# Order and pacing of an interleaved last stage: a convolution stream woven into a feed-forward network on one core

## The chip, the cores and the metric

The kernel runs on one core of one Trainium2 chip. The metric is device microseconds from one execution of the whole program; the kernel before took 1118.28 us (median of 3 runs, 1117.45 to 1119.73). The engines are named as in the profile: PE (TensorE), DVE (VectorE), ACT (ScalarE), POOL (GpSimd), SP (SyncE, which here only issues DMAs).

## What is computed

With S = 2048 positions, D = 576 channels and Dff = 4608, all in float32:

```python
xn  = layernorm(q)                          # over the 576 channels
h   = relu(xn @ w1) @ w2                    # feed-forward, 576 -> 4608 -> 576
kv  = shift_conv4(k, shift_k) * v           # 4-tap causal convolution per channel
y   = causal_conv(kv, ssm_k) + kv * ssm_D   # 2048 taps per channel, by a Fourier transform
out = q + xn * y + h
```

## The kernel before

**Two programs in one.** The feed-forward network (FFN) is the main loop, and the convolution is a generator, `conv()`, whose steps are issued in between. Positions are cut into 16 tiles t of 128 rows; four tiles make a block b, two blocks a half. Dff is cut into 12 chunks of 384, and each half goes through all of them, so that chunk numbers ci run from 0 to 11 for the first half (tiles 0 to 7) and from 12 to 23 for the second (tiles 8 to 15).

**The FFN.** Per chunk and block, `mm1` (L304) makes three hidden tiles of 128x512 with 14 matmuls each into the PSUM pool `psh` (two buffers); ACT writes the rounded relu `hh` (L319) and DVE the remainder `ll` (L320). `mm2` (L323) makes, for each of the four tiles, two products of 128x288 with 9 matmuls each into the PSUM pool `pso` (three buffers). DVE adds each product to `acc[t]`, which starts as x, in one operation that multiplies by `rstd` on the way (L337): xn is only centred before the matmuls (`centred`, L185), and the scale comes late, which relu allows. Weights come by SP (L267 to L282) and are split into a rounded and a rest part by ACT and POOL (L289, L297, L262). `make_xT` (L237) takes statistics on DVE, centres x, transposes it on PE into the PSUM pool `psf` (three buffers, shared with the convolution) and splits it. For block 2 it works in place.

**The convolution**, in four stages, each with an SBUF pool of its own; the matmuls of all of them write to `psf`:
- `fk`: first transform of the filter (L369), 32 units, to DRAM as zk.
- `fx`: four taps and a gate on DVE (L454 to L463), first transform of the result (L369), to DRAM as zx.
- `fm`: spectral product, 32 groups. For each group: k's transform (6 matmuls, L533), four copies by ACT for each half of the columns (L556 to L559); x's transform (6 matmuls), two `sw` copies by ACT (L583, L584) and a product by DVE for each half (L585), then a second product (L587) and the sum (L563); `yh` on ACT (L564) and `yl` on DVE (L566); and, a group later, the inverse transform (6 matmuls) and `vo` on ACT (L573), stored to DRAM as zy (L578). Inputs are split into `hi` by ACT and `lo` by DVE (L523, L524).
- `fo`: last transform. For tile t and u = 0, 1: load of zy (L598), `ohi` by ACT (L617) and `olo` by DVE (L618), two matmuls for each half of the columns (L657, L658), a copy by ACT (L659) and a sum by DVE (L660) into y. Then `gate(t)` multiplies by the centred x (L625) and `add(t)` scales by rstd and adds (L632): for tiles 0 to 7 to the saved first half (`fin` in DRAM) and straight to the output, on POOL's DMA queue; for tiles 8 to 15 into `acc[t]`, which the FFN of the second half is still adding to. The first transform of zy for any tile needs every group's store.

**What sets the order.** `tick` (L685) is called twice in each `mm1` and `mm2` with the matmul columns just issued. It adds `rate * cost` to a balance and, when the balance is not negative and no pause runs, takes one step of the generator; the step's weight (W_FK, W_FX, W_FM, W_FO) is taken off the balance. `rate` is the total weight of the convolution over `SHARE` of the FFN's columns less pauses (L678). At the first of the last chunk's sums in the second half, `rest_of_stream` (L343) issues whatever is left. A scheduler then places these instructions on the engines' queues: each engine runs its own queue strictly in the order given, and an instruction on the same tile as an earlier issued one waits for it. So the *issue* order decides who must wait for whom, and the scheduler, which takes what it holds to be ready, where each instruction stands on its engine.

**The start.** 22 matmuls on zeros (L715) run on PE while x and the first weights arrive; then come the transposes of the first four tiles (L231) and the first `mm1`.

Of the kernel before, what the change touches and what calls it, by code (L numbers as in the profile page):

```python
# [10 lines left out]
F32 = mybir.dt.float32  # L11
F32R = mybir.dt.float32r
AF = mybir.ActivationFunctionType
OP = mybir.AluOpType
# [24 lines left out]
GR = P // (2 * A2)  # L39
NG = A1 // GR  # L40
N_WARM = 22


W_MM1 = 14 * 512
# [63 lines left out]
def h3_ffn_kernel(ctx: ExitStack, tc, x, k, v, shift_k, ssm_k, ssm_D, w1, w2, fwd, inv, mid, out):  # L108
# [76 lines left out]
    def centred(dst, src, t):  # L185


        return nc.vector.tensor_scalar(dst, src, mv[:, t, 0:1], None, op0=OP.subtract)
# [20 lines left out]
    def first_xT(srcs):  # L209

        xT_tiles(0)
        ps = []
        for c in range(5):
            ps.append(ps_o.tile([P, 512], F32, tag="o", name=f"psx{c}") if c >= 3 else fft_psum())
        neg = xp.tile([P, BT], F32, tag="neg", name="neg", bufs=1)
        behind = None
        for t in range(BT):
            if t % 2 == 0:
                pair = xp.tile([P, 2, D], F32, tag="xn", name=f"xn{t}", bufs=BT // 2)
            xn = pair[:, t % 2, :]  # L220
            with tc.issue_after(behind.ins) if behind else nullcontext():
                stats(t, srcs[t])
                if t % 2 == 0:
                    behind = nc.vector.tensor_scalar(neg[:, t:t + 1], mv[:, t, 0:1], -1.0, None,
                                                     op0=OP.mult)
                    nc.scalar.activation(xn, srcs[t], AF.Identity, bias=neg[:, t:t + 1])
                else:
                    behind = centred(xn, srcs[t], t)
            for c in range(5):
                w = min(P, D - c * P)  # L230
                nc.tensor.transpose(ps[c][:w, t * P:(t + 1) * P], xn[:, c * P:c * P + w], ident)  # L231
        for c in range(5):
            split_x(0, c, ps[c])
        with tc.issue_after(done["dve"].ins):
            inv_std(0, BT)

    def make_xT(b, srcs, in_place=False):  # L237

        xT_tiles(b)
        t0 = b * BT  # L240
        with tc.issue_after(done["dve"].ins):
            for t in range(t0, t0 + BT):
                stats(t, srcs[t])
# [56 lines left out]
        return last  # L300

    hid = {}

    def mm1(ci, b, j):  # L304
        h1, l1, _, _ = weights[ci][j]
# [17 lines left out]
    def mm2(ci, b, i):  # L323
        t = b * BT + i
        cols = slice(i * P, (i + 1) * P)
        for h in range(2):
            ps = ps_o.tile([P, 512], F32, tag="o", name=f"pso{ci}_{t}_{h}")
            dc = slice(h * NH, (h + 1) * NH)
            n = 0
            for j in range(FT):  # L330
                hh, ll = hid[ci, b, j]
                _, _, h2, l2 = weights[ci][j]
                for a, m in ((hh, h2), (hh, l2), (ll, h2)):
                    nc.tensor.matmul(ps[:, :NH], a[:, cols], m[:, dc],  # L334
                                     start=n == 0, stop=n == 3 * FT - 1)
                    n += 1
            done["acc"] = nc.vector.scalar_tensor_tensor(  # L337
                acc[t][:, dc], ps[:, :NH], rstd[:, t:t + 1], acc[t][:, dc],
                op0=OP.mult, op1=OP.add)
# [12 lines left out]


# [25 lines left out]
    def conv():  # L379
# [212 lines left out]
        with tc.tile_pool(name="fo", bufs=2) as fp:  # L592
            raw, parts, rest, ys = {}, {}, {}, {}

            def load_z(t, u):
                if t < T:
                    raw[t, u] = fp.tile([P, D], F32, tag="zt", name=f"zo{t}_{u}", bufs=4)
                    nc.sync.dma_start(raw[t, u], zy[:, T * u + t, :])  # L598

            def load_rest(t):  # L600
                if t < T:
# [8 lines left out]
                    rest[t] = w, xt, ft  # L610

            def split(t, u):
                if t < T:
                    hi = fp.tile([P, D], F32R, tag="hi", name=f"ohi{t}_{u}", bufs=3)
                    lo = fp.tile([P, D], F32R, tag="lo", name=f"olo{t}_{u}", bufs=3)
                    with here():
                        nc.scalar.activation(hi, raw[t, u], AF.Copy)  # L617
                        nc.vector.tensor_tensor(lo, raw[t, u], hi, OP.subtract)  # L618
                    parts[t, u] = hi, lo

            def gate(t):

                if t >= 0:
                    with here():
                        nc.vector.scalar_tensor_tensor(ys[t], rest[t][1], mv[:, t, 0:1], ys[t],  # L625
                                                       op0=OP.subtract, op1=OP.mult)

            def add(t):
                if t >= 0:
                    to, more = (ys[t], rest[t][2]) if t < HT else (acc[t], acc[t])  # L630
                    with here():
                        nc.vector.scalar_tensor_tensor(to, ys[t], rstd[:, t:t + 1], more,  # L632
                                                       op0=OP.mult, op1=OP.add)
                    if t < HT:
                        move(to, out, t, store=True, queues=(nc.gpsimd, nc.gpsimd))

            units = [(t, u) for t in range(T) for u in range(U)]
            for n in range(3):
                load_z(*units[n])
            for t in range(2):  # L640
                load_rest(t)
            yield -PAUSE
            split(0, 0)
            yield -PAUSE / 8
            for n, (t, u) in enumerate(units):
                w = rest[t][0]
                hi, lo = parts[t, u]
                own, other = halves(u)
                if u == 0:
                    ys[t] = fp.tile([P, D], F32, tag="y", name=f"y{t}", bufs=3)  # L650
                low = fp.tile([P, D], F32, tag="low", name=f"low{t}_{u}")
                for h in range(2):

# [3 lines left out]
                    nc.tensor.matmul(ps[:, :NH], w[:, u, :], hi[:, cols], start=True, stop=False)  # L657
                    nc.tensor.matmul(ps[:, :NH], w[:, u, :], lo[:, cols], start=False, stop=True)  # L658
                    nc.scalar.activation(low[own, cols], ps[other, :NH], AF.Copy)  # L659
                    nc.vector.tensor_tensor(ys[t][own, cols], ps[own, :NH], low[own, cols],  # L660
                                            OP.add)
                    if h == 0:
                        if n + 1 < len(units):
                            split(*units[n + 1])
                        if n + 3 < len(units):
                            load_z(*units[n + 3])
                    else:
                        (gate if u == 0 else add)(t - 1)
                        if u == 0:
                            load_rest(t + 2)  # L670
                    yield W_FO
            gate(T - 1)
            add(T - 1)
# [36 lines left out]
    table = const.tile([P, 1], F32, name="table")  # L710
    nc.vector.memset(table, 1.0)
    nc.scalar.activation(table, table, AF.Sqrt)
    idle = fft_psum()
    for i in range(N_WARM):
        nc.tensor.matmul(idle, warm[:, :P], warm, start=True, stop=True)  # L715
    split_w1(0, 0)
    first_xT(acc)
    for j in range(1, FT):
# [80 lines left out]
```

## Time and profile before

| what | us |
|---|---|
| median of 3 runs | 1118.28 |
| the profiled execution's own time | 1114.96 |
| its span, first to last instruction | 1113.2 |
| PE busy in the span | 1080.5 |
| DVE busy | 737.3 |
| ACT busy | 583.5 |
| POOL busy | 265.4 |

Times in the rows are microseconds from the start of the span, if not marked ns. A row of the timeline has the start, the duration, the engine, the line of the kernel, the operation, then output<-inputs and their shapes, the count, and in brackets how long the engine stood idle before it and what ended that. Matmuls overlap, so that the mean duration of one is more than the distance between two. PEclk is the clock that TensorE was granted, as a share of full speed.

### The profile page before, as it was taken

Reading aid. Unit: us, or ns where it says so; the run is one execution under the profiler, and the core shown is the slowest. Engines: PE = TensorE matmul, PEld = TensorE weight load, DVE = VectorE, ACT = ScalarE, POOL = GpSimd, SP = SyncE. Lnnn points to the kernel's source line nnn. Section 1 sums busy time; section 2 is a strip of 40 time slices with the busy share of each in tenths; the row PEclk is TensorE's granted clock in tenths of the full one; section 3 lists DMA queues with packets and bytes.
Section 4 is the critical chain, followed back from the end, with each engine's and each line's share of the span. In section 5 each row is a group of like instructions: output and inputs, shape, how many; then the busy total and the mean of one; then the engine's idle time right before and its main releaser. Section 6 shows DMA issues by size and latency. Waiting matters only on the chain.

```text
span 1113.2 us, 17349 instructions
## 1 busy us (share of the span) xinstructions
PE 1080.5 (97%) x6534; PEld 980.5 (88%) x6534; DVE 737.3 (66%) x1215; ACT 583.5 (52%) x1180; POOL 265.4 (24%) x215
## 2 busy tenths in 40 slices
PE   8999999999999999999999999999999999998698
PEld 5889999988898988999989999999999999997587
DVE  6353876759999999358555654655555655468985
ACT  4221778713433343357566665676656666545540
POOL 3230331412412313303121131220312302214200
PEclk9999999999999999999999999999999999999699
DMA  9940464664544533426544133342342412288823
GB/s 236 175 144 1 145 192 138 191 184 140 178 145 152 180 118 130 142 75 201 175 132 132 54 122 99 96 121 64 121 123 63 131 54 90 89 247 248 232 73 86
DMA packets 112640, 150.79 MB, mean 135 GB/s; under 512 B 45229, under 2 KB 63279, under 8 KB 112556
## 3 DMA queue, kind: packets, MB, share of 16 engines
q1 hardware_dynamic: 104572, 135.98, 41.2%
q0 software_dynamic: 7824, 13.11, 4.5%
q8 instruction: 51, 0.84, 0.3%
q10 hardware_dynamic: 160, 0.59, 0.2%
q14 instruction: 33, 0.27, 0.1%
HBM read 114.26 MB, written 35.39 MB: 134 GB/s over the span
## 4 chain that ended last, share of the span: by engine, by line
PE 69%; DVE 16%; DMA 6%; issue 4%; ACT 3%; SPq 1%; POOL 1%; DVEq 0%; ACTq 0%; POOLq 0%
PE pso L334 30%; PE psh L314 29%; PE psf L533 6%; DVE e L457 4%; DVE acc L337 3%; DVE c L458 3%; DMA r<-in_w 2%; PE psf L369 2%; DVE ll L320 1%; DVE xs L363 1%; DVE c L454 1%; SPq L392 1%; DVE c L463 1%; DMA k-1_2411<-in_k 1%; POOL l L262 1%
## 5 line engine op out<-in xcount | busy, mean ns | idle before, releaser
L262 POOL TENSOR_TENSOR l<-r,h 128x640 fp32r<-128x640 f32 (+1 forms) x144 | 229.5, 1609 | 646.6 <-ACT h L297 318.7
L334 PE MATMUL pso<-h,hh 128*128 128x288 f32 x1152 | 339.0, 296 | 7.9 <-DVE acc L337 7.6
L334 PE MATMUL pso<-l,hh 128*128 128x288 f32 x1152 | 339.2, 295 | 0.0
L334 PE MATMUL pso<-h,ll 128*128 128x288 f32 x1152 | 338.9, 295 | 0.0
L337 DVE SCALAR_TENSOR_TENSOR acc<-pso,rstd,acc 128x288 f32<-128x288 f32 x384 | 193.4, 512 | 90.1 <-PE pso L334 88.3
L334 PEld LDWEIGHTS pso<-h,hh 128*128 128x128 f32 x1152 | 216.3, 188 | 17.4 <-DVE acc L337 11.3
L314 PE MATMUL psh<-xhi,h 128*128 128x512 f32 x576 | 226.7, 394 | 1.5 <-DVE ll L320 1.1
L314 PE MATMUL psh<-xlo,h 128*128 128x512 f32 x576 | 226.2, 393 | 0.0
L314 PE MATMUL psh<-xhi,l 128*128 128x512 f32 x576 | 225.6, 392 | 0.0
L334 PEld LDWEIGHTS pso<-l,hh 128*128 128x128 f32 x1152 | 216.8, 188 | 5.3
L334 PEld LDWEIGHTS pso<-h,ll 128*128 128x128 f32 x1152 | 216.7, 188 | 0.7
L320 DVE SCALAR_TENSOR_TENSOR ll<-psh,hh 128x512 fp32r<-128x512 f32 x144 | 98.6, 686 | 123.2 <-ACT hh L319 122.9
L319 ACT ACTIVATE hh<-psh 128x512 fp32r<-128x512 f32 x144 | 85.1, 593 | 141.4 <-PE psh L314 139.8
L314 PEld LDWEIGHTS psh<-xhi,l 128*128 128x128 f32 x576 | 108.5, 188 | 21.7
L314 PEld LDWEIGHTS psh<-xhi,h 128*128 128x128 f32 x576 | 108.3, 188 | 18.4 <-DVE ll L320 1.6
L314 PEld LDWEIGHTS psh<-xlo,h 128*128 128x128 f32 x576 | 108.5, 188 | 15.9 <-DVE xlo L203 0.4
L289 ACT ACTIVATE h<-r 128x640 fp32r<-128x640 f32 x72 | 52.4, 734 | 62.8 <-PE psh L314 30.4
L297 ACT ACTIVATE h<-r 128x576 fp32r<-128x576 f32 x72 | 46.9, 678 | 52.7 <-DMA r<-in_w 29.1
L585 DVE TENSOR_TENSOR k<-psf,k 128x288 f32<-128x288 f32 x64 | 29.1, 455 | 66.8 <-ACT sw L584 66.6
L583 ACT ACTIVATE sw<-psf 64x288 f32<-64x288 f32 x64 | 26.1, 408 | 88.9 <-PE psf L533 87.7
L314 PE MATMUL psh<-xhl,l 128*128 128x512 f32 x144 | 56.5, 392 | 0.0
L314 PE MATMUL psh<-xhl,h 128*128 128x512 f32 x144 | 56.2, 391 | 0.0
(104 smaller groups left out, 1414.3 us busy)
## 6 DMA issues: line engine op xcount, KB each, us to landing
r<-in_w SPq DMA_DIRECT2D x24, 864.0 KB, 6.6
r<-in_w SPq DMA_DIRECT2D x23, 768.0 KB, 5.6
zk<-zk SPq DMA_DIRECT2D x32, 288.0 KB, 2.4
zx<-zx SPq DMA_DIRECT2D x32, 288.0 KB, 2.4
ztk<-zk SPq DMA_DIRECT2D x32, 288.0 KB, 2.8
ztx<-zx SPq DMA_DIRECT2D x32, 288.0 KB, 2.8
zy<-vo SPq DMA_DIRECT2D x32, 288.0 KB, 2.2
zo<-zy SPq DMA_DIRECT2D x32, 288.0 KB, 3.5
```

Of the source, the lines that this page charges most:

```text
L262: return nc.gpsimd.tensor_tensor(dst, src, hi, OP.subtract)
L289: nc.scalar.activation(h1, r1[:, :, cols], AF.Copy)
L297: nc.scalar.activation(h2, r2[:, j, :], AF.Copy)
L314: nc.tensor.matmul(ps, a, m, start=i == 0, stop=i == len(seq) - 1)
L319: done["act"] = nc.scalar.activation(hh, ps, AF.Relu)
L320: nc.vector.scalar_tensor_tensor(ll, ps, 0.0, hh, op0=OP.max, op1=OP.subtract)
L334: nc.tensor.matmul(ps[:, :NH], a[:, cols], m[:, dc], start=n == 0, stop=n == 3 * FT - 1)
L337: done["acc"] = nc.vector.scalar_tensor_tensor(acc[t][:, dc], ps[:, :NH], rstd[:, t:t + 1], acc[t][:, dc], op0=OP.mult, op1=OP.add)
L457: nc.vector.tensor_tensor(e, win[t - n], sk[:, n, :], OP.mult)
L458: nc.vector.tensor_tensor(sums[t], sums[t], e, OP.add)
L533: nc.tensor.matmul(ps[:, :NH], a, m[:, cols], start=n == 0, stop=n == 2)
L585: nc.vector.tensor_tensor(k1[:, cols], ps, k1[:, cols], OP.mult)
```

## The change

- **Order of `fo`.** Tiles 8 to 15 come first, then tiles 0 to 7. Pieces are numbered by their place in that order. `add(t)` of a tile from 8 on notes the tile in `added`, and `mm2` of the last chunk takes steps of the stream until its tile is in `added`. `rest_of_stream` is no longer called there; it is still called at the very end.
- **Pacing.** SHARE goes from 0.95 to 0.985, and the weights become 1.4, 4.1, 1.26 and 2.4 (from 1.6, 3.7, 1.8 and 2.1).
- **Scale.** `make_xT`, which makes blocks 1, 2 and 3, now normalizes (centres and scales by rstd) before the transposes. `mm2` multiplies by rstd for block 0 alone; for the others DVE's sum is a plain `tensor_tensor`. In place (block 2 and 3), the statistics are now issued after the FFN's latest sum.
- **Warm-up.** 11 more matmuls on zeros, 0, 6, 3 and 2 of them issued after the transposes of the first four tiles; they write to a `psh` buffer where the 22 wrote to `psf`.
- **Output of tile 15** goes out in two halves of the columns, each on SP's and ACT's DMA queues.

Where the pacer's arithmetic places steps, as a share of the FFN's columns:

| step issued | before | after |
|---|---|---|
| `fk` begins | 0.105 | 0.105 |
| `fx` begins | 0.237 | 0.237 |
| `fm` begins | 0.453 | 0.517 |
| `fo` begins | 0.818 | 0.822 |
| `add(8)` | 0.897 | 0.833 |
| `add(15)` | at the end of the stream, 0.948 | 0.903 |
| stream ends | 0.948 | 0.983 |

The diff, cut to its core:

```diff
@@ constants
+WARM_TILE = (0, 6, 3, 2)
-SHARE = 0.95
+SHARE = 0.985
-W_FK, W_FX, W_FM, W_FO = 1.6, 3.7, 1.8, 2.1
+W_FK, W_FX, W_FM, W_FO = 1.4, 4.1, 1.26, 2.4
@@ first_xT, after the transposes of tile t
+            keep_warm(WARM_TILE[t])
@@ make_xT
-        with tc.issue_after(done["dve"].ins):
+        with tc.issue_after(done["acc" if in_place else "dve"].ins):
-            centred(xn[-1], srcs[t], t)
+            normalized(xn[-1], srcs[t], t)
@@ mm2
+        if ci == HALVES * NCHUNK - 1:
+            while t not in added:
+                next(stream)
-            done["acc"] = nc.vector.scalar_tensor_tensor(
-                acc[t][:, dc], ps[:, :NH], rstd[:, t:t + 1], acc[t][:, dc],
-                op0=OP.mult, op1=OP.add)
+            if b == 0:
+                done["acc"] = nc.vector.scalar_tensor_tensor(
+                    acc[t][:, dc], ps[:, :NH], rstd[:, t:t + 1], acc[t][:, dc],
+                    op0=OP.mult, op1=OP.add)
+            else:
+                done["acc"] = nc.vector.tensor_tensor(acc[t][:, dc], ps[:, :NH], acc[t][:, dc],
+                                                      OP.add)
+            if ci == HALVES * NCHUNK - 1 and t == T - 1:
+                for u, queue in ((0, nc.sync), (1, nc.scalar)):
+                    queue.dma_start(out[u, :, t, dc], acc[t][halves(u)[0], dc])
-            if t >= HT:
-                rest_of_stream()
-                if t >= T - 2:
+                if t == T - 2:
-                elif t % 2:
+                elif t % 2 and t < T - 1:
@@ conv, stage fo
+            order = [*range(HT, T), *range(HT)]
+            units = [(t, u) for t in order for u in range(U)]
...
+                    else:
+                        added.add(t)
...
-            units = [(t, u) for t in range(T) for u in range(U)]
@@ start
-    idle = fft_psum()
-    for i in range(N_WARM):
-        nc.tensor.matmul(idle, warm[:, :P], warm, start=True, stop=True)
+    idle = ps_h.tile([P, 512], F32, tag="h", name="psw")
+
+    def keep_warm(n):
+        for i in range(n):
+            nc.tensor.matmul(idle, warm[:, :P], warm, start=True, stop=True)
+
+    keep_warm(N_WARM)
```

More of the change, by code (lines that the diff above doesn't have):

```diff
@@ L302, in h3_ffn_kernel @@
     hid = {}
+    added = set()
     def mm1(ci, b, j):
@@ L609, in load_rest, with split, gate, add @@
                         nc.sync.dma_start(ft, fin[t // 2, :, t % 2, :])
[L610 to L615, printed above, removed]
[L616 to L623 removed]
+                    rest[i] = w, xt, ft
+            def split(n):
+                if n < len(units):
+                    hi = fp.tile([P, D], F32R, tag="hi", name=f"ohi{n}", bufs=3)
+                    lo = fp.tile([P, D], F32R, tag="lo", name=f"olo{n}", bufs=3)
+                    with here():
+                        nc.scalar.activation(hi, raw[n], AF.Copy)
+                        nc.vector.tensor_tensor(lo, raw[n], hi, OP.subtract)
+                    parts[n] = hi, lo
+            def gate(i):
+                if i >= 0:
+                    t = order[i]
                     with here():
[L625 removed]
+                        nc.vector.scalar_tensor_tensor(ys[i], rest[i][1], mv[:, t, 0:1], ys[i],
                                                        op0=OP.subtract, op1=OP.mult)
[L628 to L630 removed]
+            def add(i):
+                if i >= 0:
+                    t = order[i]
+                    to, more = (ys[i], rest[i][2]) if t < HT else (acc[t], acc[t])
                     with here():
[L632 removed]
+                        nc.vector.scalar_tensor_tensor(to, ys[i], rstd[:, t:t + 1], more,
                                                        op0=OP.mult, op1=OP.add)
```

41 lines of the change are left out of this document (21 added, 20 removed).

## The prediction

> **What bounds the kernel now.** I read the page's slices first, then busy time by stage, then what PE waited for, then the timelines of the worst stage.
>
> ```profile
> PE   8999999999999999999999999999999999998698
> PEclk9999999999999999999999999999999999999699
> ```
>
> PE is full from slice 2 to slice 36. What is lost lies in slices 37 to 39. Busy time by stage (columns: stretch, its length, then busy time and count on PE, PEld, DVE, ACT, POOL; PE clock; DMA share, GB/s):
>
> ```profile
> 14.00:17.30 3.30, 3.30 (x9) 2.30 (x9) 3.24 (x6) 3.30 (x7) 2.77 (x3) 0.51 1.02 229
> 240.00:440.00 200.00, 194.81 (x1173) 176.28 (x1172) 190.77 (x261) 75.87 (x145) 58.94 (x44) 1.00 0.49 151
> 600.00:900.00 300.00, 300.00 (x1858) 276.81 (x1857) 167.44 (x284) 194.13 (x416) 62.99 (x41) 1.00 0.34 103
> ...
> 1026.00:1049.00 23.00, 12.35 (x41) 8.78 (x40) 22.01 (x39) 14.44 (x32) 6.55 (x12) 0.61 0.91 268
> 1049.00:1066.00 17.00, 13.86 (x82) 12.34 (x82) 16.58 (x31) 9.80 (x21) 1.59 (x3) 0.92 0.65 182
> ```
>
> In the spectral product (600 to 900) no engine but PE is full. In the last transform (1026 to 1066) DVE is, and PE runs 41+82 matmuls in 40 us. What one costs when nothing waits, from the chain of work that ended last:
>
> ```profile
> 1090.42 18.15 PE pso L334 x135
> ```
>
> That is 0.134 us, so 123 matmuls are worth 16.5 us and the stage loses 23.5 us. PE's waits name DVE (waits in 1000 to 1066, 240 to 440, 60 to 80; us in total, times, longest):
>
> ```profile
> PE psf L657 <- DVE y L660: 14.9, 14, 1.5
> ...
> PE pso L334 <- DVE acc L337: 5.2, 6, 1.6
> ...
> PE pso L334 <- DVE acc L337: 2.4, 1, 2.4
> ```
>
> Why PE has only last-stage matmuls to run there is in the timeline of DVE, and then PE:
>
> ```profile
> 1036.77 0.82 DVE L632 SCALAR_TENSOR_TENSOR y<-y,rstd,ft 128x576 f32<-128x576 f32 x1
> 1037.50 0.75 DVE L618 TENSOR_TENSOR olo<-zo,ohi 128x576 fp32r<-128x576 f32 x1
> 1038.29 0.94 DVE L660 TENSOR_TENSOR y<-psf,low 64x288 f32<-64x288 f32 x2
> ...
> 1039.82 0.80 DVE L625 SCALAR_TENSOR_TENSOR y<-xt,mv,y 128x576 f32<-128x576 f32 x1
> ...
> 1041.52 0.82 DVE L632 SCALAR_TENSOR_TENSOR y<-y,rstd,ft 128x576 f32<-128x576 f32 x1
> ...
> 1046.26 0.82 DVE L632 SCALAR_TENSOR_TENSOR acc<-y,rstd,acc 128x576 f32<-128x576 f32 x1
> ...
> 1048.27 0.94 DVE L337 SCALAR_TENSOR_TENSOR acc<-pso,rstd,acc 128x288 f32<-128x288 f32 x2
> ```
>
> ```profile
> 1034.06 0.61 PE L657 MATMUL psf<-ohi,wi 128*128 128x288 f32 x1 [1.16 <-DVE y L660]
> 1034.46 0.45 PE L658 MATMUL psf<-olo,wi 128*128 128x288 f32 x1
> 1034.70 0.45 PE L657 MATMUL psf<-ohi,wi 128*128 128x288 f32 x1
> ...
> 1048.94 0.51 PE L334 MATMUL pso<-h,hh 128*128 128x288 f32 x1
> ```
>
> One tile takes 4.75 us of DVE (1036.77 to 1041.52). At 1046.26 comes the first add that writes acc, tile 8. Only behind it do DVE's sums of the FFN into acc[8] run (1048.27), and only then does PE get an FFN product (1048.94). **The lock:** add(8) was issued before chunk 22's sum into the same tile, so that sum waits for it; the pool pso has three buffers, so PE's FFN stops after three products.
>
> **The change part by part.** *New order of the last stage, new weights.* The pacer's arithmetic (front part) places the last stage's start at 0.822 of the FFN's work, 0.818 before. But tile 8 is now first: its add is issued at 0.833, before chunk 20's sums, where it stood at 0.897, before chunk 22's. The lock moves two chunks forward. I read off the changed kernel's instruction order what PE meets there. The spectral product runs late against its issue, as it does before, and is 5.5 groups from its end. Chunk 20's products for tile 8 and half of tile 9 fill pso; then PE has 99 spectral matmuls in a row, 20 of the last stage, and only then the next FFN product. In the old order spectral matmuls come between FFN products to the end. On DVE, behind the waiting sum, stand the FFN's other sums and ll; for these waits PE's FFN and, through it, the weight splits on ACT and POOL.
>
> What the run of 99 costs is not in the trace, since there the FFN fills its waits. ACT's and DVE's groups in 600 to 900 (last: busy us, mean ns | idle before):
>
> ```profile
> L558 ACT ACTIVATE k<-psf 64x288 f32<-64x288 f32 x40 | 16.3, 408 | 0.5
> ...
> L583 ACT ACTIVATE sw<-psf 64x288 f32<-64x288 f32 x39 | 15.9, 408 | 63.3 <-PE psf L533 62.5
> ...
> L523 ACT ACTIVATE hix<-ztx 128x576 fp32r<-128x576 f32 x20 | 13.7, 687 | 0.5
> ...
> L573 ACT ACTIVATE vo<-psf 128x288 f32<-128x288 f32 x38 | 13.5, 408 | 0.5
> L564 ACT ACTIVATE yh<-k 128x576 fp32r<-128x576 f32 x20 | 13.5, 673 | 0.0
> ```
>
> ```profile
> L566 DVE TENSOR_TENSOR yl<-k,yh 128x576 fp32r<-128x576 f32 x20 | 21.8, 1090 | 11.2 <-ACT yh L564 11.2
> L585 DVE TENSOR_TENSOR k<-psf,k 128x288 f32<-128x288 f32 x39 | 17.7, 455 | 49.0 <-ACT sw L584 49.0
> ...
> L563 DVE TENSOR_TENSOR k<-k,k 128x576 f32<-128x576 f32 x20 | 15.0, 750 | 0.0
> L587 DVE TENSOR_TENSOR k<-sw,k 128x576 f32<-128x576 f32 x20 | 15.0, 749 | 0.0
> ```
>
> A group has on ACT eight k copies and four sw copies at 0.41, two hi at 0.69, two vo at 0.41 and yh at 0.67: 7.7 us. ACT must also wait twice: after yh, for the five matmuls up to x's first product (at the half clock of PE's rows 0.40, then 0.24 apart: 1.6 us), and before the second sw pair, whose product needs the PSUM buffer that vo has just freed (0.5 us). A cycle is 9.8 us. The 99 are 9 matmuls that end a group (6.9 us to its yh), four cycles of 18 (9.8, 9.8, then 9.1 and 8.4 as splits run out), 12 without k copies (sw, DVE's 0.46+0.75+0.75, yh: 7.2) and 6 (yl, four matmuls, vo: 2.8): **54 us**. From below it is ACT's busy time alone, 38.7. From above, the pace of the trace, 39 sw copies for 19.5 groups in 300 us, 15.4 a group: 78.
>
> Then the stage hand-over, bare now (SP, and ACT's first hi of the last stage):
>
> ```profile
> 974.60 0.33 SPq L578 DMA_DIRECT2D zy<-vo  x1
> 976.84 1.28 SPq L598 DMA_DIRECT2D zo<-zy  x3
> ...
> 979.77 0.69 ACT L617 ACTIVATE ohi<-zo 128x576 fp32r<-128x576 f32 x1 [3.98 <-DMA zo<-zy]
> ```
>
> From the last store to the first hi, 5.2 us. Before chunk 20's first sum frees a buffer, DVE has six olo (0.75), seven y sums (0.47), a gate (0.80), an add (0.82) and that sum (about 0.46): 9.9 us behind a hi of 0.7, say 11. So PE stands on 119 matmuls for 54+5.2+11 = 70 us; their own worth is 16: **54 lost**. Until the next products of the FFN's first half, DVE has 14.4 us of work for 74 matmuls, 9.9 us: 4 lost, and 1.5 for the half clock on return, as at 1049. Sum **+60**. The old stage's 23.5 go. After that the last stage lies beside two and a half chunks (nothing charged but 1 for single waits; at 4.75 us a tile DVE has room there, and uncovered it would be the old 23.5). Its DMAs move with it: zo, xt and ft loads on SP stand among weight loads with the FFN's slack, and the first half's 16 stores on POOL now come last, but some 20 us before the end, when POOL has no weights to split. The new wait loop of chunk 23 asks for nothing: tile 15's add is issued by 0.903.
>
> *Clock in that run.* The trace's stage fell to 0.61 with no PE wait over 1.5 us, so I use half clock. The Trainium skill, "TensorE: Matmul & The Clock Gate", section "Why this matters for your kernels", asks only that idle gaps stay under about 3 us. By that the run would keep full speed, each cycle would be about 0.9 us shorter and the sum 4 us less; this trace speaks against it.
>
> *Second transform stretched* (from 0.237-0.437 to 0.237-0.501 of the FFN). DVE's 190.77 us in 200 spread over some 264. Of 5.2 us of PE waits I take back 4, since the order keeps its first part dense; bounds 0 and 5.2.
>
> *Statistics of block 2* wait for the FFN's latest sum (in_place): they leave the 60 to 80 stretch, whose 2.4 us wait goes, and come at the end of the second transform, just ahead of their transposes. Bounds 0 and a like wait there; I take −2.4 and +0.5.
>
> *Late scaling for block 0 only.* 288 of 384 sums lose their scalar. Nearest rows: L585 at 455 ns against
>
> ```profile
> L337 DVE SCALAR_TENSOR_TENSOR acc<-pso,rstd,acc 128x288 f32<-128x288 f32 x384 | 193.4, 512 | 90.1 <-PE pso L334 88.3
> ```
>
> so 16 us less on DVE, hidden by PE wherever DVE is not full, and part of the second transform's gain. Block 1 now needs rstd before its transposes; these moved behind chunk 0's third hidden tile. I cost it at 0; uncovered it is a few small DVE steps, 1 us.
>
> *Warm-up.* Start of the trace:
>
> ```profile
> 1.20 7.88 PE L715 MATMUL psf<-warm 128*128 128x512 bf16 x22 [1.20 <-DVE table L711]
> ...
> 11.42 0.55 PE L231 MATMUL psf<-ident,xn 128*128 128x128 f32 x3 [1.25 <-ACT xn L226]
> ...
> 12.70 0.55 PE L231 MATMUL psf<-ident,xn 128*128 128x128 f32 x3 [0.51 <-DVE xn L188]
> ```
>
> In the new order 32 of the 33 stand before the first transpose. They end about 2.1 us later than 9.1, so the transposes fill both gaps and the last ends some 0.3 us later. The half clock of 14.0 to 17.3 costs half of 3.3 us, 1.7. If it stays full: −1.4; if not: +0.3. PE is now busy nearly throughout the 3 us before, so −1.4. The Trainium skill, "TensorE: Matmul & The Clock Gate", section "Part 4: PE-mode transpose", holds that transposes do not count as activity for the clock. By that it would fall, and the sum would be 1.7 more.
>
> *Output of tile 15 by halves on two queues*: one issue less behind the last sum, −0.5 (0 to −1).
>
> **Sum:** +60 − 23.5 + 1 − 4 − 1.9 − 1.4 − 0.5 = **+29.7** on the profiled execution's 1114.96 us (span 1113.2): 1144.7. The median of the runs, 1118.28, lies 3.3 above; rounded, I forecast **1148**.
>
> **The rivals.** *Work-bound run (lower):* ACT's waits overlap and 38.7 stands for 54: 1133. For it, ACT has no idle before most groups of 600 to 900; against it, L583's 63.3 us of idle behind PE. *Slow run (higher):* 15.4 a group for the four cycles adds 24: 1172. That pace is the order's, not a limit, which speaks against it. *Faster:* the change does what its words say: the second half's adds land before anyone needs them, there is no run of 99, the old 23.5 go and the small gains stay: 1088. It decides at chunk 20's fourth product: the spectral product must be over by then, which asks for 5.5 groups of some 13 to 15 us less delay. The order speaks against it; faster stages on the chip cannot help, since PE takes its queue in order.
>
> **How the numbers follow.** Forecast 1139 to 1158: 0.57. Work-bound, 1125 to 1139: 0.21. Slow, 1158 to 1180: 0.16. Faster: 0.05; within 0.2% by the meeting of all low ends: 0.01. The range 1131 to 1166 leaves out the tails and the faster case. A measurement here tells about 0.2% from no change. Faster 0.05, same 0.01, slower 0.94.
>
> **What would show it.** After: one stretch of some 70 us near 920 to 990 with PE a quarter busy, clock near 0.5, ACT near full, then 11 us of DVE; the first sum into acc[8] of chunk 20 right behind the add; no burst at 1026. PE waits of 240 to 440 near 1 us; none at 70. Clock 1.0 at 14 to 17. I am wrong if FFN products run between the spectral matmuls there, or if the stretch is under 50 us.

## The result and the profile after

The changed kernel takes **1151.95 us** (median of 4 runs, 1149.64 to 1154.19); the kernel before, run beside it, 1119.01 (1117.45 to 1121.66). The ratio is 1.0292, 95% interval 1.0262 to 1.0321: slower by 32.9 us, where the prediction had 29.7.

The page's slices of the changed kernel:

```profile
span 1150.5 us, 17358 instructions
...
PE   8899999999999999999999999999999964499998
...
PEclk9999999999999999999999999999999976599999
```

Three slices of PE, 28.8 us each, are at 6, 4 and 4 where all before them from the third on were at 9: from 920 to 1006. The burst in the last slices of the kernel before is gone. Busy time by stage (columns as in the prediction):

```profile
14.00:17.30 3.30, 3.30 (x14) 2.41 (x14) 3.24 (x6) 3.30 (x7) 2.73 (x3) 1.00 1.03 236
240.00:440.00 200.00, 199.13 (x1200) 180.96 (x1199) 170.01 (x242) 70.80 (x132) 56.70 (x41) 1.00 0.46 139
...
928.00:984.00 56.00, 26.42 (x100) 22.41 (x98) 22.45 (x36) 37.56 (x87) 0.00 (x0) 0.63 0.15 48
984.00:1002.00 18.00, 7.72 (x22) 5.56 (x23) 9.87 (x18) 8.31 (x17) 2.67 (x5) 0.50 0.95 281
```

The third row is the run of spectral matmuls: 100 matmuls in 56 us, ACT busy for 37.6 of them. The fourth is the hand-over to the last stage and its start: 22 matmuls in 18 us. PE's own timeline, cut to the first spectral matmul of the run, the rows with a wait of over 3 us and the first FFN product behind:

```profile
927.84 0.30 PE L544 MATMUL psf<-hix,m_sb 128*128 128x288 f32 x1
...
934.51 0.85 PE L544 MATMUL psf<-yh,m_sb 128*128 128x288 f32 x2 [5.31 <-ACT yh L575]
...
944.68 0.85 PE L544 MATMUL psf<-yh,m_sb 128*128 128x288 f32 x2 [4.95 <-ACT yh L575]
...
954.85 0.85 PE L544 MATMUL psf<-yh,m_sb 128*128 128x288 f32 x2 [4.91 <-ACT yh L575]
...
964.44 0.85 PE L544 MATMUL psf<-yh,m_sb 128*128 128x288 f32 x2 [4.30 <-ACT yh L575]
...
973.47 0.85 PE L544 MATMUL psf<-yh,m_sb 128*128 128x288 f32 x2 [3.53 <-ACT yh L575]
...
981.17 0.85 PE L544 MATMUL psf<-yh,m_sb 128*128 128x288 f32 x2 [3.64 <-ACT yh L575]
...
990.30 1.06 PE L679 MATMUL psf<-ohi,wi 128*128 128x288 f32 x3 [7.01 <-DMA zo<-zy]
...
1001.66 0.45 PE L340 MATMUL pso<-h,hh 128*128 128x288 f32 x1
```

The starts of the yh rows stand 10.2, 10.2, 9.6, 9.0 and 7.7 us apart: one cycle of the spectral product after the other, each with PE waiting for ACT. Then the hand-over (SP's queue, then ACT):

```profile
983.76 0.32 SPq L589 DMA_DIRECT2D zy<-vo  x1
986.00 1.27 SPq L615 DMA_DIRECT2D zo<-zy  x3
```

```profile
988.94 0.68 ACT L635 ACTIVATE ohi<-zo 128x576 fp32r<-128x576 f32 x1 [5.20 <-DMA zo<-zy]
```

and on DVE the add that writes acc[8], with the FFN sums right behind it:

```profile
998.31 0.80 DVE L652 SCALAR_TENSOR_TENSOR acc<-y,rstd,acc 128x576 f32<-128x576 f32 x1
999.03 1.43 DVE L636 TENSOR_TENSOR olo<-zo,ohi 128x576 fp32r<-128x576 f32 x2
1000.50 0.46 DVE L682 TENSOR_TENSOR y<-psf,low 64x288 f32<-64x288 f32 x1
1000.99 0.82 DVE L348 TENSOR_TENSOR acc<-pso,acc 128x288 f32<-128x288 f32 x2
```

0.67 us after the sum starts, PE has an FFN product (1001.66, above). PE did without the FFN from 927.84 to 1001.66, 73.8 us.

**A common measure for all runs.** DVE makes 384 sums of FFN products, in the same order in each kernel. For the n-th, counted from 0, I take its start in the trace and subtract what the matmuls ahead of the last one of its product in PE's instruction order need at full pace: 0.1335 us for 288 columns (0.134 in the prediction), 0.229 for 512, warm-up included, 0.11 for a transpose. What remains is the time that PE has lost so far, however the convolution is spread; a sum's wait in DVE's queue, between 0.3 and 5.5 us at these sums, is in the figure too. In us:

```
sum                24    96   180   228   312   348   last   span   measured median
before           12.7  15.1  22.7  21.7  18.6  20.1  43.7  1113.2  1119.0
after            11.9  13.4  12.9  13.2  12.8  79.6  79.3  1150.5  1152.0
old_order        13.1  15.4  14.5  14.7  14.6  14.1  55.3  1126.5  1127.2
old_pace         13.5  16.2  22.3  24.2  22.6  60.5  59.1  1130.3  1132.1
order_alone      10.2  14.2  21.1  20.5  17.4  63.4  60.5  1129.2  1132.2
pace_alone       11.8  16.8  18.2  20.9  17.5  17.8  72.5  1141.2  1143.2
defer            14.6  18.0  17.1  17.4  17.1  16.8  17.7  1121.3  1121.8
psum24            8.0  20.0  28.0  35.3  37.9  40.4  39.5  1110.7  1112.5
psum24_before    13.3  24.2  34.0  35.9  37.0  36.2  36.5  1106.0  1112.0
scale_alone      10.3  11.8  17.6  21.1  19.5  22.4  39.5  1108.2  1107.4
warm_alone       13.1  15.7  22.6  22.5  19.5  19.8  43.4  1114.6  1117.5
repace_old_order 11.1  13.9  17.7  18.8  16.2  19.1  27.0  1098.2  1098.8
repace_defer     14.5  17.6  21.1  23.5  20.9  22.5  21.7  1094.3  1095.2
repace_new_order 12.3  14.7  18.2  18.9  16.7  48.3  46.9  1118.1  1120.8
```

Sums 24 to 228 span the first and second transform, 312 to 348 the place of the lock in the new order, 348 to the last that of the old burst. In the changed kernel 66.8 us go between sums 312 and 348, and nothing after; in the kernel before 23.6 go behind sum 348. The steps from 96 to 228 also show what the second transform costs: 6.6 before, nothing after.

### The profile page after: what moved, and what is told of

It reads as the page before. It is cut to its first block, busy times and chain, and to the rows that moved or that the text cites. A ratio compares the mean times of both kernels' runs of the same rounds, so it can differ in the third digit from the quotient of the medians.

```text
span 1150.5 us, 17358 instructions
## 1 busy us (share of the span) xinstructions
PE 1093.3 (95%) x6545; PEld 992.2 (86%) x6545; DVE 714.9 (62%) x1215; ACT 588.4 (51%) x1180; POOL 263.3 (23%) x215
## 4 chain that ended last, share of the span: by engine, by line
PE 82%; DMA 5%; ACT 5%; DVE 3%; SPq 2%; issue 2%; POOL 1%; ACTq 0%; DVEq 0%
PE psh L317 35%; PE pso L340 35%; PE psf L544 6%; PE psf L380 3%; DMA r<-in_w 2%; SPq L403 1%; DMA zo<-zy 1%; POOL l L264 1%; DVE e L468 1%; DMA sk<-in_shift_k 1%; PE psf L679 1%; PE psf L680 1%; ACT k L569 0%; ACT k L570 0%; DVE c L469 0%
## 5 line engine op out<-in xcount | busy, mean ns | idle before, releaser
L348 DVE TENSOR_TENSOR acc<-pso,acc 128x288 f32<-128x288 f32 x288 | 128.1, 451 | 70.5 <-PE pso L340 67.9
L291 ACT ACTIVATE h<-r 128x640 fp32r<-128x640 f32 x72 | 52.4, 735 | 70.0 <-DMA r<-in_w 38.7
L299 ACT ACTIVATE h<-r 128x576 fp32r<-128x576 f32 x72 | 46.7, 680 | 77.6 <-DMA r<-in_w 44.3
L344 DVE SCALAR_TENSOR_TENSOR acc<-pso,rstd,acc 128x288 f32<-128x288 f32 x96 | 47.8, 511 | 28.1 <-PE pso L340 27.3
L544 PE MATMUL psf<-yh,m_sb 128*128 128x288 f32 x128 | 36.2, 331 | 26.7 <-ACT yh L575 26.6
```

The lines of the kernel that those rows point to most:

```text
L291: nc.scalar.activation(h1, r1[:, :, cols], AF.Copy)
L299: nc.scalar.activation(h2, r2[:, j, :], AF.Copy)
L344: done["acc"] = nc.vector.scalar_tensor_tensor(acc[t][:, dc], ps[:, :NH], rstd[:, t:t + 1], acc[t][:, dc], op0=OP.mult, op1=OP.add)
L348: done["acc"] = nc.vector.tensor_tensor(acc[t][:, dc], ps[:, :NH], acc[t][:, dc], OP.add)
L544: nc.tensor.matmul(ps[:, :NH], a, m[:, cols], start=n == 0, stop=n == 2)
```

## The experiments

**Theory (lag and lock).** An add of the last stage into acc[t] is issued before FFN sums into the same tile. If PE's instruction order still holds convolution matmuls of earlier stages there, the FFN stops after pso's three buffers and these matmuls run bare. **Rival (work).** The later spectral product and the last stage are bound by ACT and DVE; the loss is theirs in any order, and without the lock it only moves.

**The new order undone** (1127.18 us; ratio to before 1.0066, 1.0042 to 1.0091):

```diff
-            order = [*range(HT, T), *range(HT)]
+            order = [*range(T)]
```

> The changed kernel with the last stage's tiles in the old order 0 to 15; pace, warm-up, scaling and the rest stay new. Theory (lock): with the second half's tiles last, add(8) comes after the spectral product is over, so the run of spectral matmuls goes; in the instruction order 80 last-stage matmuls then stand in a row before chunk 22's sums of tile 9. At 4.75 us of DVE a tile of 8 matmuls, less 0.134 us each, that loses 0.46 us a matmul, some 37 to 40 us against 23.5 in the kernel before: about 1127 us, one stretch of some 45 us near the end with DVE full and the clock low, and no gaps for yh. Rival (work: a spectral stage issued later and faster is bound by ACT and must be paid in any order): 1145 or more, with ACT nearly full in the lost stretch.

As the lock theory had it, to a microsecond. The run is gone (sums 312 to 348 lose nothing) and the old burst is back, longer: 41.2 us behind sum 348 against 23.6. Its waits (1000 to 1085) and its busy time:

```profile
PE psf L679 <- DVE y L682: 21.0, 22, 2.7
```

```profile
1014.00:1082.00 68.00, 46.23 (x184) 35.50 (x183) 60.54 (x108) 37.34 (x80) 15.83 (x29) 0.65 0.89 272
```

PE waits for the last stage's sums, DVE is busy for 60.5 of 68 us, the clock is at 0.65. ACT is busy for little more than half of the time, and of PE's waits it ends one, of 0.6 us.

**The old pace under the new order** (1132.14 us; 1.0113, 1.0087 to 1.0139):

```diff
-SHARE = 0.985
+SHARE = 0.95
-W_FK, W_FX, W_FM, W_FO = 1.4, 4.1, 1.26, 2.4
+W_FK, W_FX, W_FM, W_FO = 1.6, 3.7, 1.8, 2.1
```

> The changed kernel with the old SHARE 0.95 and the old four weights; the new order of the last stage stays. Theory (lock): the spectral product starts earlier in the FFN, and the run of matmuls before the locked sum is 36 spectral and 20 last-stage ones instead of 99 and 20. 36 cost two cycles of 7 to 10 us and the end of 2.8, some 20 us; with the hand-over 5.2 and the ramp 11 that is 36 us standing, 34 lost with the recovery, against 23.5 before: about 1126 us. Rival (the new order itself costs what it costs, since the lock comes two chunks earlier whatever the pace): about 1148 to 1152.

Between the two, nearer to the lock theory, 6 us more than it had. 37.9 us go at the lock where I expected 34. And the old pace costs by itself in the second transform: 8 us between sums 96 and 228, 0 at the new pace. PE's waits at the lock (930 to 1030):

```profile
PE psf L544 <- ACT yh L575: 7.8, 2, 4.2
PE psf L679 <- DMA zo<-zy: 6.9, 1, 6.9
PE psf L679 <- DVE y L682: 4.8, 3, 2.5
```

Two cycles' waits for yh instead of six, and the same bare hand-over.

**The new order alone on the kernel before** (1132.16 us; 1.0152, 1.0122 to 1.0182). The diff of `fo` and `mm2` as shown above, with all else old:

> The kernel before with the new order of the last stage (8 to 15, then 0 to 7) and the output of tile 15 by halves; old pace, weights, warm-up and scaling. Theory (lock): here 45 spectral and 20 last-stage matmuls stand before the locked sum of chunk 20. From the two kernels measured (99 and 20: about 69 us lost at the lock; 36 and 20: about 37) a spectral matmul in the run costs 0.52 us, so about 41 lost against some 25 in the kernel before: 1135 us. Rival (the order is harmless at the old pace; only pace and order together lock): 1119.

3 us under the expectation, far from the rival. The new order locks at the old pace too; 46.0 us go at the lock. PE's waits there (930 to 1030):

```profile
PE psf L544 <- ACT yh L575: 11.9, 3, 4.8
PE psf L679 <- DMA zo<-zy: 8.8, 1, 8.8
```

**The new pace alone on the kernel before** (1143.24 us; 1.0238, 1.0213 to 1.0263). SHARE and weights as in the change, all else old:

> The kernel before with SHARE 0.985 and the new weights (and the output of tile 15 by halves); old order, warm-up and scaling. Theory (lag and lock): in the instruction order 6 spectral and 86 last-stage matmuls stand before chunk 22's sum of tile 9, against 44 in the kernel before and 80 in the changed kernel with the old order, which lost about 45 us there against some 30. With 0.41 us for each more and a bare hand-over of up to 5 that is 48 to 53 lost, +18 to +23; the stretched second transform gives 4 to 7 back: 1131 to 1136 us. Rival (pace is harmless in the old order; the harm is the new order's alone): 1110 to 1117.

The direction is the theory's, the size is not: 7 us over its upper end. 54.7 us go behind sum 348. PE's waits (990 to 1100):

```profile
PE psf L679 <- DVE y L682: 20.2, 20, 1.9
PE psf L679 <- DMA zo<-zy: 7.3, 1, 7.3
PE psf L679 <- ACT ohi L635: 3.3, 2, 2.7
PE psf L544 <- ACT yh L575: 2.5, 1, 2.5
```

The spectral product is so late here that the hand-over is bare behind the lock in the old order as well: 7.3 and 3.3 us, where I had allowed 5.

**Adds deferred** (1121.78 us; 1.0026, 1.0010 to 1.0043). The changed kernel, with y kept until the last chunk (cut; four of the eight tiles lie in buffers that are free by then, four in new ones, and zt and the statistics' q have a buffer less):

```diff
@@ add(t), t from 8 on
-                        nc.vector.scalar_tensor_tensor(to, ys[i], rstd[:, t:t + 1], more, ...)
+                        added[t] = ys[i]
@@ mm2 of the last chunk, after its wait loop
+            nc.vector.scalar_tensor_tensor(acc[t], added[t], rstd[:, t:t + 1], acc[t], ...)
```

> The changed kernel, but the last stage keeps its results for tiles 8 to 15 in buffers of their own (four in buffers that are free by then, four more; one zt buffer less), and adds each to acc just before chunk 23's sum into that tile. Nothing is left out. Theory (lock): no FFN sum before chunk 23 waits for the last stage, so FFN products run between the spectral matmuls to their end and the run of 99 goes; the last stage then runs out over the FFN's end, 56 of its matmuls (7 tiles at 4.75 us, 33 us, less their own 7.5) behind the last FFN product: 26 lost at the end in place of 23.5 at the old burst, so about 1115 us, gaps for yh gone, a burst in the last 35 us. Rival (ACT and the stage's own work bound it; the lock only shows it): 1140 or more, PE still waiting for yh between 900 and 1000.

The deciding one. With no FFN sum before chunk 23 behind an add, the curve stays flat at 17 to 18 from sum 96 to the last: no gap for yh, no loss around 930 to 1000. PE's waits from 900 to the end:

```profile
PE psf L687 <- DVE y L690: 16.2, 16, 3.5
PE psf L546 <- DVE yl L579: 0.5, 1, 0.5
```

ACT had no trouble with the squeezed spectral product; 30 us of the changed kernel's time are gone with the work unchanged. What remains stands behind the last FFN sum, 7 us dearer than expected. The 56 matmuls themselves took 33.8 us (1076.0 to 1109.8), as expected, although the clock was low; but from the start of the last matmul to the end of the span it is 11.4 us here (last sums, gate, add, store), against 4.1 in the changed kernel, and this tail had not been charged:

```profile
1078.00:1121.00 43.00, 16.80 (x50) 11.58 (x50) 31.88 (x56) 16.93 (x36) 10.80 (x20) 0.55 0.75 217
```

**PSUM buffers 2 and 4** (on the changed kernel: 1112.46 us; 0.9944, 0.9925 to 0.9962. On the kernel before: 1112.04; 0.9972, 0.9956 to 0.9988):

```diff
-    ps_o = ctx.enter_context(tc.tile_pool(name="ps_o", bufs=3, space=PSUM))
-    ps_f = ctx.enter_context(tc.tile_pool(name="ps_f", bufs=3, space=PSUM))
+    ps_o = ctx.enter_context(tc.tile_pool(name="ps_o", bufs=2, space=PSUM))
+    ps_f = ctx.enter_context(tc.tile_pool(name="ps_f", bufs=4, space=PSUM))
```

> The changed kernel with one PSUM buffer moved: two for the FFN's products (pso), four for the convolution's (psf). Theory (lag): three psf buffers, not the engines, make the spectral product lag its issue; with four it ends in the instruction order some 30 us of PE earlier, before add(8) is issued, and no run of convolution matmuls is left. Then the case the words of the change describe: 1114.96 - 23.5 - 4 - 1.9 - 1.4 - 0.5, with 3.3 up to the median: about 1087 us, if two buffers are enough for the FFN; each FFN product takes nine matmuls, 1.2 us, and DVE's sum 0.46, so waits for acc come where DVE is near full (240 to 460): up to 1100. Rival (work-bound): 1140 or more, the loss of 54 us still near 930 to 1000 or at the end.

> The kernel before with two PSUM buffers for the FFN's products and four for the convolution's. The burst at 1026 goes in the instruction order, 24 us. What the third pso buffer was worth is the question: in the changed kernel with 2 and 4, PE lost 15.5 us of busy time between 200 and 560 against the changed kernel with 3 and 3. Theory (the FFN needs three buffers where DVE is near full, and the old pace fills DVE more in the second transform): 1118 to 1130, the gain paid back before 560. Rival (the loss there belongs to the changed pace): 1095 to 1100.

The mechanism is as expected, the times are not: the first is 12 us over its upper end, the second lies between theory and rival. With the buffer moved, the spectral product keeps its pace: the lock loses 2.5 us instead of 66.8, without any other edit, and the old burst goes from the kernel before as well. So the lag goes with the sharing of the PSUM buffers, not with the engines' work. Whether the fourth psf buffer removed it, or the FFN that two pso buffers slow down, these runs do not separate. The FFN paid for it: 25 us lost by sum 312 beyond the changed kernel's, and 18 beyond the kernel before's. Busy time of PE, psum24 and then the changed kernel:

```profile
200.00:560.00 360.00, 343.59 (x2055) 310.31 (x2055) 259.94 (x409) 125.30 (x239) 88.83 (x68) 0.99 0.46 140
```

```profile
200.00:560.00 360.00, 359.13 (x2181) 327.53 (x2181) 272.60 (x427) 140.56 (x266) 99.48 (x73) 1.00 0.50 151
```

15.5 us of PE are missing there. I had bounded that cost at 13 us in all; by sum 312 it was 25.

**Scaling alone on the kernel before** (1107.41 us; 0.9908, 0.9886 to 0.9931). The diff of `make_xT` and of `mm2`'s sums:

> The kernel before with the late scaling for block 0 only and the statistics of the second half's blocks behind the FFN's sums (and the output of tile 15 by halves); old order, pace and warm-up. In the instruction order 30 instead of 44 last-stage matmuls stand in the row before the locked sum. If that row is what costs (0.41 us each), 6 less; the statistics 2: 1108 to 1111 us. If the scalar was hidden by PE and nothing else moves: 1114 to 1117.

Faster, by as much as expected or a little more. PE's wait in the burst (1000 to 1066), to be set against 14.9 us in the kernel before:

```profile
PE psf L679 <- DVE y L682: 7.9, 9, 1.2
```

The instruction order changes with this edit, 30 matmuls in the row of the old burst instead of 44, and 17.1 us go behind sum 348 where it was 23.6. That is enough for the two traces (spans 1108.2 and 1113.2); the medians differ by 11.5, and the rest of that is not accounted for. Nor is the shorter row separated from the DVE time that the plain sums save in the burst, where DVE is near full, so that the row as the cause is argued, not shown.

**Warm-up alone on the kernel before** (1117.47 us; 0.9997, 0.9981 to 1.0014):

> The kernel before with the eleven warm-up matmuls behind the first transposes (and the output of tile 15 by halves); all else old. Theory (the half clock of 14.0 to 17.3 goes, 1.4, and the output gives 0.5): 1115 us, the first sum of the FFN some 1.3 us earlier. Rival (the gain is eaten within 80 us by weights that arrive no earlier): 1117, the first sum earlier, the loss at 80 us the same.

No difference that can be told. The clock at the start is the new one, 1.00 in place of 0.51:

```profile
14.00:17.30 3.30, 3.28 (x13) 2.43 (x14) 3.24 (x6) 3.30 (x7) 2.78 (x3) 1.00 1.01 229
```

The first FFN product starts at 21.17 us, 1.1 earlier than in the kernel before. But from 33.4 to 36.9 us the clock is 0.51, where it is 1.00 in the kernel before, and no FFN sum is gained by 290 us. DVE's busy time in the sums and their count, here (L344) and in the kernel before (L337):

```profile
0.00:290.00 290.00, 48.34 (x96) 0.99 0.56 152
```

```profile
0.00:290.00 290.00, 48.39 (x97) 0.99 0.57 155
```

ACT waits longer for the next weights instead (20 to 60 us; the longest of these waits here, then the same line's in the kernel before; with L299 and L297 it is 9.7 us against 5.7):

```profile
ACT h L291 <- DMA r<-in_w: 7.2, 1, 7.2
```

```profile
ACT h L289 <- DMA r<-in_w: 2.5, 1, 2.5
```

**Another pace** (old order 1098.76 us, 0.9847, 0.9822 to 0.9872; new order with adds deferred 1095.19, 0.9816, 0.9792 to 0.9840; new order 1120.77, 1.0058, 1.0037 to 1.0080). The changed kernel with

```diff
-SHARE = 0.985
+SHARE = 0.95
-W_FK, W_FX, W_FM, W_FO = 1.4, 4.1, 1.26, 2.4
+W_FK, W_FX, W_FM, W_FO = 1.2, 4.0, 1.8, 2.1
```

> The changed kernel with the old order of the last stage, SHARE 0.95 and the weights 1.2, 4.0, 1.8, 2.1: the first transform's columns are issued faster, the second's slower than before, the spectral product ends in the instruction order some 14 to 20 us of PE before it does with the old weights. Nothing is left out, no buffer is moved. Theory (lag and lock): add(8) then meets a convolution that is on time; no run of more than 13 convolution matmuls is left in the order. The lock's loss goes, some 25 us of before: 1118.6 - 25 - 2 to 7 for warm-up and second transform: 1087 to 1095 us, no slice of PE under 9 from 920 to 1070. Rival (DVE's 4.75 us a tile and ACT bound the end anyway): 1110 or more, with PE waiting for y of the last stage.

> The same pace, with the new order of the last stage and the second half's results kept in buffers and added in chunk 23. By the lock theory no FFN sum waits before chunk 23 at all; the last stage ends some 15 us of PE later than with the old order, just ahead of the end. 1087 to 1097 us, within 5 us of the same pace with the old order. Rival (work at the end): 1105 or more, a burst in the last 20 us.

> The changed kernel with SHARE 0.95 and the weights 1.2, 4.0, 1.8, 2.1, and its new order of the last stage, without buffers of its own for the second half. In the instruction order 9 spectral and 20 last-stage matmuls are left before the locked sum (99, 45 and 36 spectral ones in the kernels measured, which lost 67, 46 and 38 us there). If the run is the price alone, 9 spectral matmuls cost what three waits cost and the time is near that of the old order at the same pace, 1099 to 1103 us. If the hand-over (5 us from store to load and split, bare) and the ramp of 11 us of DVE stand behind any run, the loss is about 24 us, 13 more than the old order at the same pace: 1109 to 1115 us.

The first transform is issued faster, so that the spectral product starts and ends earlier and the second transform is still stretched. Two of the three **beat both kernels**, with deferred adds by 1.8% against before; the old order is 4 us over its expectation. With deferred adds no slice of PE is under 9 between the second and the last (page's slices), and DVE, at 63.1 of 70 us, is near full at the end without stopping PE:

```profile
PE   8799999999999999999999999999999999999998
```

```profile
1020.00:1090.00 70.00, 69.08 (x444) 64.39 (x443) 63.10 (x116) 28.58 (x59) 18.26 (x25) 1.00 0.61 175
```

In the old order 4.0 us of waits for y remain, and 8 us go behind sum 348. The third kernel is a miss and tells most: with only 9 spectral matmuls left ahead of the locked sum, the lock still takes 31.6 us (sums 312 to 348), where the higher of the two expectations had 24; the time is 6 us over that one's upper end. PE's longest waits there (900 to 1030):

```profile
PE psf L679 <- DMA wi<-in_inv: 8.7, 1, 8.7
PE psf L544 <- ACT yh L575: 3.6, 1, 3.6
PE psf L679 <- DVE y L682: 3.1, 4, 1.8
```

One wait for yh is left, and the hand-over as bare as ever. Here the last to arrive was not zy but wi, the transform's matrix, whose load POOL issues only behind the last store of zy: 8.3 us from that store (949.01) to PE's first last-stage matmul (957.26), 6.5 in the changed kernel (983.76 to 990.30). Four kernels in the new order, by the spectral matmuls ahead of the locked sum: 9, 36, 45 and 99 cost 31.6, 37.9, 46.0 and 66.8 us. On a straight line through these four some 27 us are there whatever the run, and 0.4 us come with each spectral matmul.

## Why the prediction was right, point by point

**The lock (+60, measured 66.8).** Place and course were as forecast. The run: 54 us forecast, 55.9 from 927.84 to the store at 983.76. Its cycles are 10.2, 10.2, 9.6, 9.0 and 7.7 against 9.8, 9.8, 9.1, 8.4 and 7.2: each 0.4 to 0.6 more, in the same steps. The hand-over: 5.2 forecast, 5.2 from 983.76 to 988.94. The ramp: 11, measured 12.7 to PE's first FFN product. 73.8 us standing less 119 matmuls at 0.134 are 57.9; the return took the other 8.9, where 5.5 had been charged.

**The work-bound and the slow run** both fall: 38.7 would have shown ACT full, and it was busy for 37.6 of 56 us; 15.4 us a group shows in no cycle of the run. That the lock is the cause, and not the stage's work, is shown by the deferred adds. Three of the prediction's own signs were off, though: in the 73.8 us the clock was 0.60, not near 0.5, PE was busy for 34.0 us, not for a quarter, and ACT for 45.8 us, not near full. The sum does not rest on ACT being full; it had ACT wait in every cycle.

**The old stage (−23.5)** lost 25.1 us behind sum 312 in the kernel before. It went entirely.

**The second transform (−4).** Between sums 96 and 312 the kernel before lost 3.5 us and the changed one gained 0.6 back: −4.1. PE is busy for 199.13 us of 200 where it was 194.81.

**The start (−3.8: warm-up −1.4, wait for the statistics −2.4)** is the step that failed: +0.7. Sum 96 comes at 290.5 us, at 289.8 before, with the same matmuls ahead but for the 11 of the warm-up, which are 2.5 us themselves. Both effects are there: the clock is full from 14.00 to 17.30, the first FFN product starts at 20.96 us instead of 22.30, and the 2.4 us wait at 70 is gone. Two things take them back. PE waits 4.3 us for hh between 20 and 90 in the changed kernel (0.2 before), behind ACT's waits for weights:

```profile
ACT h L299 <- DMA r<-in_w: 8.3, 1, 8.3
ACT h L291 <- DMA r<-in_w: 7.0, 1, 7.0
```

And the half clock comes back. Behind a stretch with PE busy for 1.23 of 3.3 us (28.0 to 31.3), the clock is 0.50 for 3.4 us, about as long as the stretch that went at 14. The changed kernel, then the kernel before:

```profile
31.30:34.70 3.40, 3.40 (x14) 2.96 (x13) 3.03 (x6) 1.17 (x3) 1.18 (x1) 0.50 1.01 162
```

```profile
31.30:34.70 3.40, 3.40 (x20) 2.93 (x19) 2.09 (x4) 0.10 (x1) 1.22 (x1) 1.00 1.11 178
```

Of the nine kernels with the new warm-up, eight have a stretch at half clock that starts between 28 and 50 us; of the five with the old one, none has. So the prediction looked for what hides a saving on PE and not for what PE meets earlier: weights that arrive no sooner, and a half clock that follows the wait for them. The 0.7 itself is the difference of two single traces; kernels with the same start reach sum 24 up to 3.5 us apart. But the sign is firm: sum 24, ahead of which no kernel has convolution matmuls, comes at 91.3, 92.9 and 93.8 us in three kernels with the old start, at 94.7 to 98.2 in the seven of the same PSUM split with the whole new one, and at 96.7 with the warm-up alone. Whether the statistics' part came by itself is open: "Scaling alone", which has it with the old warm-up, reaches sum 24 at 91.4, within what the three show without it.

As to the page of the Trainium skill that says of transposes that they do not count as PE-busy in the same way ("TensorE: Matmul & The Clock Gate", "Part 4: PE-mode transpose"): the granted clock was 1.00 at 14.00 to 17.30, so the prediction's choice of a full clock there was right, and the run goes against the reading that it would fall. In the kernel before it did fall, 0.51, behind the same transposes; the runs do not settle the page's statement.

**Late scaling (0).** The plain sum takes 451 ns in the mean, against the 455 taken:

```profile
L348 DVE TENSOR_TENSOR acc<-pso,acc 128x288 f32<-128x288 f32 x288 | 128.1, 451 | 70.5 <-PE pso L340 67.9
```

The price of a plain sum was right. In the kernel before, though, this edit (with the statistics') is worth 11.5 us on the medians, and the row of the old burst is shorter with it. In the changed kernel that row does not exist. The zero itself was not tried there: no run takes this edit out of the changed kernel.

**The sum.** On the two profiled executions: +66.8 at the lock, −0.3 after it, −25.1 for the old stage, −4.1, +0.7 and −0.8 behind the last sum make +37.2; the spans differ by 37.3. The forecast had 29.7; the start is 4.5 of the difference, the lock and its recovery 5.5, and the old stage takes 1.6 back. On medians the distance is 32.9, since the profiled execution of the kernel before lay 4 us below its median. That the forecast came this near on medians is in part luck: on the traces it is 7.5 us short, the lock too cheap and the start with the wrong sign.

**The faster rival** named its condition too weakly. It asked that the spectral product be over by chunk 20's fourth product. With half a group left (9 matmuls) the price was still 31.6 us: the last stage's hand-over and its first tile must be over as well, before the sum that waits for add(8) comes up. And neither half of the change is harmless alone: the new order costs 15 us, the new pace 24, both by matmuls that pile up ahead of a locked sum.

## What to carry to other kernels

When a stream of work is woven into another, look in the instruction order for the first instruction of the main work that waits for the stream, and count what of the stream still stands ahead of it: that runs bare, with the stages' hand-over and the first results' latency in full. Keep such results in a buffer until the main work no longer cares, or let the stream's middle stages come earlier; together the two made the fastest kernel. An edit that saves time on a hidden engine can still pay, or cost, by the order that it gives.

## What the runs showed of the hardware

The clock fell without long gaps again: in the burst of the kernel with the old order the longest wait of PE was 2.7 us, the granted clock 0.65. Read as enough by itself, the rule of the Trainium skill ("TensorE: Matmul & The Clock Gate", "Why this matters for your kernels": idle gaps under about 3 us) would have kept full speed; the trace disagrees. In the run of 99 the waits were 3.5 to 5.3 us and the clock 0.63, so that there rule and trace agree; the prediction, which took the rule to mean full speed in that run, had not set its own cycles of some 10 us beside it.

At the start, two waits of 1.25 and 0.51 us between transposes went with a clock of 0.51 at 14.00 to 17.30 in the kernel before; in the changed kernel, with more matmuls ahead, waits of 0.56 and 0.51 went with 1.00 (rows below). The waits alone do not tell which it will be: the new pace on the kernel before, with the old warm-up and waits of 1.67 and 0.52 us there, had 1.00 as well. Over all kernels the clock in this stretch was 0.50, 0.51, 0.70, 0.86 and 1.00 with 22 warm-up matmuls, and 1.00 in all nine with 33.

```profile
11.51 0.55 PE L232 MATMUL psf<-ident,xn 128*128 128x128 f32 x3 [0.56 <-ACT xn L227]
...
12.79 0.55 PE L232 MATMUL psf<-ident,xn 128*128 128x128 f32 x3 [0.51 <-DVE xn L189]
```

Giving the FFN's third PSUM buffer to the convolution cost the FFN of the changed kernel 25 us and that of the kernel before 18 us (lost time at sum 312), though one product takes PE nine matmuls, 1.2 us, and DVE's sum only 0.45 to 0.51 us.
